# A transfer on SyncE that waits for the last weights is taken out; early stores and dense weights queue behind the values of step 1 instead

## Chip, cores, metric

One Trainium2 chip (trn2), one core. The metric is device time in microseconds (us), the median of several executions; lower is better. Span is the length of the profiled execution alone; it is about 2 us shorter than the time of the same run.

## The reference, cut to what matters

Two kinds of layer, each twice: a recurrent attention layer (A) and a dense layer with relu (B), with residuals.

```python
def _A_ref(x, mem0, Wq, Wk, Wv, Wo, seg_len):      # x: 1 x 2048 x 512, 32 heads of 128
    mem = mem0                                     # 8 rows
    for s in range(n_seg):                         # 64 segments of 32 rows
        h = jnp.concatenate([mem, xs], axis=1)     # 40 rows
        q, k, v = h @ Wq, h @ Wk, h @ Wv           # (written as einsums)
        p = _softmax(where(mask, q k^T * scale, -1e9))
        o = (p v) @ Wo
        mem = o[:, :M, :]                          # the next segment needs it
        outs.append(o[:, M:, :])
x = x + _A_ref(_layernorm(x), ...)
x = x + relu(_layernorm(x) @ w1) @ w2
x = x + _A_ref(_layernorm(x), ...)
x = x + relu(_layernorm(x) @ w1) @ w2
```

The memory makes the segments a chain. The kernel does segment k of the first layer A and segment k - 4 of the second in one *step* k; there are 68 steps. The values of a step are put in place by transfers: its "first values" by two (`V<-vg`), its others by four (`V<-vw`). At the end of every step but the last a VectorE copy (`HT<-st`) puts the new memory where the next step's matmuls read it, so the times of these copies measure the steps.

## The kernel before: the parts that the argument touches

The weights (16 MB of Wq, Wk, Wv, Wo in bf16) are loaded once. The program is a list of operations, which a planner written in the kernel puts in order for each engine, using a table of tuned numbers; the order of each engine is then fixed. The framework that compiles the list places all semaphore waits.

```python
def load_weights():
    for c, p0, n in (...):                       # Wv in 3 parts, then Wq, Wk, Wq, Wk, Wo, Wo
        ...                                      # first part of Wv on SyncE, all others on GpSimd
    def hold():                                  # 32 bytes of the last weights, to a scratch place in DRAM
        nc.sync.dma_start(out=held[:], in_=Wo_sb[0:1, H - 1, 0:16])
    plan.op(SP, 0.78, hold, r=[("W", "o", 2), ("issued", "v", 0)], w=["loaded"], lag=0.0)

def queue(early):                                # who issues: ScalarE early, SyncE later and after "loaded"
    return (ACT, nc.scalar, 0.45, []) if early else (SP, nc.sync, 0.78, ["loaded"])

def prepare_group(g, gate=()):                   # a group is 128 rows of x; groups 1 to 5 are early (EARLY = 5)
    eng, q, t, cond = queue(g <= EARLY)
    def load():
        q.dma_start(out=xb[:, :], in_=A_x[0, 128 * g:128 * (g + 1), :])     # xe: a ring of two buffers
    plan.op(eng, t, load, r=[*cond, *gate], w=[xb], lag=...)
    xnT = layernorm(xb, ...)                     # transposes on PE, copied out by ScalarE or VectorE (xg)
    def put():                                   # the normalised group, kept in DRAM for later
        nc.sync.dma_start(out=xh[g][:], in_=xnT[:, :, :])
    plan.op(SP, 0.5, put, r=[*on(xnT), "loaded"], w=[("xh", g)], lag=3.0)
    if g <= EARLY:
        late_values(g, xnT, range(4))            # x Wv for these rows, before they are due: matmuls "fill<-Wv_sb,xg"
...
load_dense()                                     # w1, w2 of layer B, on SyncE, after "loaded"
for k in range(nsteps):
    ...                                          # load_group, prep_x, step_values, queries_keys, scores, attend,
                                                 # project, place_values, finish_pair (layer B)
```

`held` is a barrier on SyncE: a tiny transfer that reads the last weights, so that everything behind it in SyncE's order waits until they have landed. Its purpose is that stores and later loads do not compete with the weights.

Of the kernel before, what the change touches and what calls it, by code (L numbers as in the profile page):

```python
# [29 lines left out]
RULE = (0.0747, 374.3032, 410609.8064, 1181571967619443.75)  # L30
PERIOD = 67.7026
PLACE = {
    ("attend.mmu0.0", 0): 532.15, ("attend.mmu0.0", 1): -8.807, ("attend.mmu1.0", 0): 515.265,
    ("attend.mmu1.0", 1): 519.958, ("attend.mmu2.0", 0): -268.171, ("attend.mmu2.0", 1): -133.306,
    ("attend.mmu3.0", 0): 161.173, ("attend.mmu3.0", 1): -96.674, ("attend.mmu4.0", 0): -137.041,
    ("attend.mmu4.0", 1): 517.755, ("dense_layer.mm.0", 1): 921.103, ("dense_layer.mm.1", 1): -138.913,
    ("dense_layer.mm.2", 1): -30.48, ("dense_layer.mm.3", 1): 458.108, ("dense_layer.mm.4", 1): -61.608,
    ("dense_layer.mm.5", 1): 915.299, ("finish_pair.turn.0", 1): -801.919, ("g0", 0): -11.927, ("g1", 0): -283.649,
    ("g2", 0): 639.371, ("g3", 0): -139.08, ("g4", 0): 661.02, ("g5", 0): -907.409,
    ("layernorm.turn.0", 1): 227.012, ("layernorm.turn.1", 1): 293.927, ("layernorm.turnr.0", 0): -126.847,  # L40
    ("prepare.turns.0", 0): 540.383, ("project.mm.0", 0): 653.938, ("project.mm.0", 1): 333.318,
    ("project.mm.1", 0): 525.334, ("project.mm.1", 1): 334.98, ("project.mm.2", 0): -82.003,
    ("project.mm.2", 1): 518.149, ("project.mm.3", 0): -40.444, ("project.mm.3", 1): 888.541,
    ("project.mm.4", 0): 246.943, ("project.mm.4", 1): -190.689, ("queries_keys.mmu0.0", 0): -893.01,
    ("queries_keys.mmu0.0", 1): -273.831, ("queries_keys.mmu0.1", 0): -842.026,
    ("queries_keys.mmu0.1", 1): -260.974, ("queries_keys.mmu0.2", 0): -138.796, ("queries_keys.mmu0.2", 1): -4.82,
    ("queries_keys.mmu0.3", 0): -63.064, ("queries_keys.mmu0.3", 1): -125.098, ("queries_keys.mmu1.0", 0): -807.001,
    ("queries_keys.mmu1.0", 1): -900.663, ("queries_keys.mmu1.1", 0): -211.227, ("queries_keys.mmu1.1", 1): -802.87,
    ("queries_keys.mmu1.2", 0): -193.148, ("queries_keys.mmu1.2", 1): -101.071, ("queries_keys.mmu1.3", 0): 111.427,
    ("queries_keys.mmu1.3", 1): -112.736, ("queries_keys.mmu2.0", 0): 372.189, ("queries_keys.mmu2.0", 1): 202.79,  # L50
    ("queries_keys.mmu2.1", 0): 269.477, ("queries_keys.mmu2.1", 1): -102.412, ("queries_keys.mmu2.2", 0): 336.89,
    ("queries_keys.mmu2.2", 1): 125.355, ("queries_keys.mmu2.3", 0): 290.402, ("queries_keys.mmu2.3", 1): 338.394,
    ("queries_keys.mmu3.0", 0): 166.135, ("queries_keys.mmu3.0", 1): 341.493, ("queries_keys.mmu3.1", 0): 263.967,
    ("queries_keys.mmu3.1", 1): 482.48, ("queries_keys.mmu4.0", 0): 524.199, ("queries_keys.mmu4.0", 1): 677.388,
    ("queries_keys.mmu4.1", 0): 454.561, ("queries_keys.mmu4.1", 1): 484.463, ("scores.mmu0.0", 0): -71.985,
    ("scores.mmu0.0", 1): -274.011, ("scores.mmu1.0", 0): 409.078, ("scores.mmu1.0", 1): -990.128,
    ("scores.mmu2.0", 0): -27.329, ("scores.mmu2.0", 1): -82.185, ("scores.mmu3.0", 0): 355.769,
    ("scores.mmu3.0", 1): -114.427, ("scores.mmu4.0", 0): -179.163, ("scores.mmu4.0", 1): -202.683,
    ("scores.turnu0.0", 0): -96.292, ("scores.turnu0.0", 1): 407.69, ("scores.turnu1.0", 0): 458.682,
    ("scores.turnu1.0", 1): 265.886, ("scores.turnu2.0", 0): -824.161, ("scores.turnu2.0", 1): -111.663,  # L60
    ("scores.turnu3.0", 0): -254.322, ("scores.turnu3.0", 1): -268.111, ("scores.turnu4.0", 0): -113.328,
    ("scores.turnu4.0", 1): -181.523, ("values.mm.0", 0): 314.251, ("values.mm.0", 1): 239.343,
    ("values.mm.1", 0): 458.697, ("values.mm.1", 1): -169.069, ("values.mm.2", 0): -66.768,
    ("values.mm.2", 1): 323.729, ("values.mm.3", 0): 571.213, ("values.mm.3", 1): 412.559,
    ("values.mmv0.0", 0): 500.356, ("values.mmv1.0", 0): 434.514, ("values.mmv2.0", 0): 343.318,
    ("values.mmv3.0", 0): 452.783, ("values_narrow.mm.0", 0): -130.097, ("values_narrow.mm.0", 1): -716.386,
    ("values_narrow.mm.1", 0): -612.132, ("values_narrow.mm.1", 1): -220.288,
}
AHEAD = {
    "*bulk.land": -8.095, "*late_values.put": 202.39, "*layernorm.aggr": -92.722, "*layernorm.keep": 142.091,  # L70
    "*layernorm.norm": 249.576, "*layernorm.power": 243.925, "*layernorm.stats": -235.438,
    "*prepare_group.load": -371.102, "*prepare_group.put": 305.32, "*values.ev": -86.818, "attend.ev": -102.918,
    "bulk.land": -139.542, "dense_layer.relu": -63.922, "dense_layer.relu_last": 129.251,
    "finish_pair.add": -261.94, "finish_pair.add0": -215.289, "finish_pair.add1": -256.949,
    "finish_pair.store": 282.199, "finish_pair.widen": 16.832, "late_values.put": 32.946,
    "layernorm.aggr": -276.636, "layernorm.keep": 160.217, "layernorm.norm": -103.511, "layernorm.power": 80.297,
    "layernorm.stats": 44.758, "load_dense.dma1": -59.82, "load_dense.dma2": 248.765, "load_group.get": 110.148,
    "load_group.load": -176.804, "load_weights.dma": -143.99, "load_weights.hold": 53.55, "make_ident": 603.953,
    "make_mask": -111.15, "place_values.dma": -102.564, "prep_x.cp": -256.472, "prepare.get_memory": -96.462,
    "prepare.get_x": 1.615, "prepare.keep": 207.944, "prepare.make_half": -302.762, "prepare.place": -8.736,  # L80
    "prepare.zero": 266.216, "prepare.zero_bank": -152.164, "prepare.zero_columns": 393.537,
    "prepare_group.load": 227.12, "prepare_group.put": -4.216, "project.ev": 251.68, "project.first": 329.265,
    "project.rows": 90.099, "queries_keys.ev": 465.016, "scores.block": 171.381, "scores.exp": 45.003,
    "scores.keep": 73.576, "scores.mul": 297.927, "scores.recip": -327.622, "scores.sub": -127.394,
    "scores.top": -18.285, "scores.total": 62.725, "values.ev": 148.812, "values_narrow.ev": -129.376,
# [213 lines left out]
def kernel(  # L299
# [82 lines left out]
    def load_weights():  # L382

        for c, p0, n in (("v", 0, 1), ("v", 1, 1), ("v", 2, 2), *((c, p0, 2) for cc, p0 in (("qk", 0), ("qk", 2), ("o", 0), ("o", 2)) for c in cc)):
            def dma(c=c, p0=p0, n=n):
                q = nc.gpsimd if (c, p0) != ("v", 0) else nc.sync
                if c == "o":
                    hs = slice(8 * p0, 8 * (p0 + n))
                    q.dma_start(out=Wo_sb[:, hs, :], in_=A_Wo.rearrange("h e d -> e h d")[:, hs, :])
                else:  # L390
                    cs = slice(p0 * PW, (p0 + n) * PW)
                    q.dma_start(out=W_s[c][:, :, cs], in_=W_v[c][:, :, cs])

            bulk(POOL if (c, p0) != ("v", 0) else SP, 0.78, dma, (c, p0), n, w=[("W", c, p0 + i) for i in range(n)],
                 rate=LOAD_O if c == "o" else LOAD)

        def hold():
            nc.sync.dma_start(out=held[:], in_=Wo_sb[0:1, H - 1, 0:16])

        plan.op(SP, 0.78, hold, r=[("W", "o", 2), ("issued", "v", 0)], w=["loaded"], lag=0.0)  # L400

# [53 lines left out]
    held = dram.tile([1, 16], BF, name="held")  # L455
# [91 lines left out]
    hold = [None]  # L547
# [117 lines left out]
    def queue(early):  # L665

        return (ACT, nc.scalar, 0.45, []) if early else (SP, nc.sync, 0.78, ["loaded"])

    def prepare_group(g, gate=()):

        eng, q, t, cond = queue(g <= EARLY)
# [3 lines left out]
        else:  # L675
# [5 lines left out]
            plan.op(eng, t, load, r=[*cond, *gate], w=[xb], lag=SLOW if g <= EARLY else 2.45)  # L681
# [3 lines left out]
        else:  # L685
# [3 lines left out]
            plan.op(SP, 0.5, put, r=[*on(xnT), "loaded"], w=[("xh", g)], lag=3.0)  # L689
# [4 lines left out]
    def load_group(g):  # L694
# [9 lines left out]
        plan.op(SP, 0.78, get, r=["loaded", ("xh", g)], w=[xnT], lag=2.45)  # L704
        plan.op(SP, 0.78, load, r=["loaded"], w=[xb], lag=2.45)
# [89 lines left out]
    def late_values(g, xnT, ps, gate=()):  # L795
# [5 lines left out]
        for p0, n in ((0, 4),) if 0 < g <= min(EARLY, 4) else ((0, 2), (2, 2)):  # L801
# [9 lines left out]
            else:  # L811
                plan.op(SP, 0.78, put, r=["loaded", *[("vg", p) for p in range(p0, p0 + n)]], w=[("vh", g, p0)], lag=4.0)
# [44 lines left out]
    def place_values(k, late):  # L857
# [5 lines left out]
        eng, q, t, cond = queue(k == 0)  # L863
# [316 lines left out]
```

## Time and profile before

| | before |
|---|---|
| median time (the profiled execution, 1661.4 us, not counted) | 1660.28 us (1660.22 to 1660.41, 3 runs) |
| span of the profiled execution | 1659.4 us |
| PE busy | 1595.7 us (96%) |
| longest idle of PE | 26.3 us, from 28.2 to 54.55 us |
| first matmul of step 1 | 82.16 us |

The first view gives busy time by windows: start and end of the stretch, its length, busy us and instructions of PE (TensorE's matmuls), PEld (its weight loads), VectorE (DVE), ScalarE (ACT), GpSimd (POOL), then the granted clock of PE, the share of the DMA engines in use and GB/s.

```profile
core 0: us, PE busy (x) PEld busy (x) DVE busy (x) ACT busy (x) POOL busy (x), PEclk, DMA share, GB/s
30.00:50.00 20.00, 0.00 (x0) 0.00 (x0) 0.00 (x0) 0.00 (x0) 0.00 (x0) 0.50 1.02 360
526.00:1026.00 500.00, 497.09 (x12540) 430.26 (x12537) 356.75 (x947) 328.32 (x803) 41.68 (x100) 1.00 0.11 28
```

In the middle of the kernel PE is busy 99.4%. In the start, no engine computes for 20 us while the weights stream at 360 GB/s.

The waits name who released whom: engine, line and what it wrote, its releaser, total us, times, longest. First PE, ScalarE and SyncE in the first 60 us:

```profile
PE fill L827 <- ACT xg L763: 28.6, 2, 26.3
```

```profile
ACT xg L763 <- DMA held<-Wo_sb: 27.6, 1, 27.6
```

```profile
SPq L398 <- DMA Wo_sb<-in_A_Wo_dram: 51.1, 1, 51.1
```

PE waits for a copy on ScalarE, and that copy for the transfer `held`, although the copy reads nothing of it. The timeline of ScalarE shows how (start, duration, engine; ACTq is ScalarE's queue that issues transfers, in order with its compute):

```profile
25.68 0.59 ACT L763 CAST xg<-fill 128x512 bf16<-128x512 f32 x1
53.52 0.34 ACTq L679 DMA_DIRECT2D xe<-in_A_x_dram  x1
53.91 0.59 ACT L763 CAST xg<-fill 128x512 bf16<-128x512 f32 x1 [27.64 <-DMA held<-Wo_sb]
```

Ahead of the copy stands the issue of a load (L679, x of group 5), and this issue is what waited. The chain that ended last says the same (start, duration, what):

```profile
11.04 41.33 DMA Wo_sb<-in_A_Wo_dram
...
52.39 1.06 DMA held<-Wo_sb
...
53.52 0.34 ACTq L679
...
53.91 0.59 ACT xg L763
...
54.55 1.49 PE fill L827 x4
```

Why does a load of x wait for `held`? The compiled order names the semaphores that each instruction waits for. In it the framework gives the transfers that ScalarE and SyncE issue ("hardware DMAs") eight completion semaphores (DMAHW0 to DMAHW7) in rotation, both queues together: the ninth transfer takes the semaphore of the first, and is not issued until the first has landed. In ScalarE's compiled order, and at the front of SyncE's (not a view of the profile; first number: place in the engine's order):

```
ScalarE  29 L679 DMACopy xe_75<-in_A_x_dram 128x512 [waits DMAHW7_49,DVE_49]
SyncE     2 L398 DMACopy held<-Wo_sb 1x16 [waits DMASW7_49]
SyncE     3 L687 DMACopy xh_108<-xg_68 128x512 [waits DMAHW0_49,DVE_49]
```

`held` is the eighth hardware DMA by this rotation, so it has DMAHW7, and the load of x is the sixteenth. (DMASW7 is the last weight load, on GpSimd.)

At 95.4 us all compute engines stop for 2 us with no releaser ("issue"), while the dense weights load at a DMA share of 1.03:

```profile
97.43 0.57 PE L1046 MATMUL st<-OT,Wo_sb 128*128 128x40 bf16 x16 [2.06 <-issue]
```

### The profile page before, as it was taken

The numbers are of one execution on the slowest core, as the hardware profiler recorded it, in microseconds if no ns is written. First come the engines' busy times: TensorE is split into PE (matmuls) and PEld (weight loads), VectorE is DVE, ScalarE is ACT, GpSimd is POOL, SyncE is SP. The second block draws the span as 40 slices with busy tenths as digits, with TensorE's granted clock in tenths as the row PEclk, the third lists the DMA queues.
The fourth block names the chain that finished last, engine by engine and source line by source line (L and its number), as shares of the span: only waits on it lengthen the run. The fifth ranks groups of instructions, "written<-read, shape, count | busy, mean of one in ns | idle before, by whom it ended". The sixth has DMA issues, their size and how long they took to land.

```text
span 1659.4 us, 89728 instructions
## 1 busy us (share of the span) xinstructions
PE 1595.7 (96%) x40624; PEld 1371.5 (83%) x40624; DVE 1122.4 (68%) x3107; ACT 1049.3 (63%) x2633; POOL 146.1 (9%) x352
## 2 busy tenths in 40 slices
PE   3699999999999999999999999999999999999998
PEld 2478888888888888888888888888888888888886
DVE  3256776677677677767776776676677667766765
ACT  2456676666666666666666666676666666666664
POOL 3101010000000010000000000000000000000000
PEclk8799999999999999999999999999999999999999
DMA  9431101010010111001010101011010010000000
GB/s 356 156 105 28 29 25 31 25 34 22 22 35 24 31 32 25 18 27 35 24 31 25 34 21 31 22 29 32 24 41 18 21 28 26 18 18 19 18 6 7
DMA packets 35488, 64.30 MB, mean 39 GB/s; under 512 B 7226, under 2 KB 19234, under 8 KB 35106
## 3 DMA queue, kind: packets, MB, share of 16 engines
q1 hardware_dynamic: 29218, 39.09, 8.8%
q0 software_dynamic: 4704, 18.35, 3.0%
q8 instruction: 318, 5.21, 1.4%
q10 hardware_dynamic: 1184, 1.12, 0.3%
q14 instruction: 64, 0.52, 0.1%
HBM read 33.50 MB, written 11.93 MB: 27 GB/s over the span
## 4 chain that ended last, share of the span: by engine, by line
PE 93%; DMA 3%; DVE 2%; ACT 1%; issue 1%; POOL 0%; ACTq 0%; POOLq 0%; DVEq 0%
PE work L907 37%; PE st L1046 18%; PE fill L827 16%; PE fill L533 11%; PE work L1019 4%; PE work L936 4%; DMA Wo_sb<-in_A_Wo_dram 2%; PE work L533 2%; ACT OT L763 0%; DVE HT L1062 0%; PE fill L642 0%; DMA xe<-in_A_x_dram 0%; PE fill L846 0%; ACT PT L1000 0%; ACT es L958 0%
## 5 line engine op out<-in xcount | busy, mean ns | idle before, releaser
L907 PE MATMUL work<-HT,Wq_sb 128*128 128x80 bf16 (+1 forms) x8704 | 368.3, 200 | 9.9 <-DVE HT L1062 9.1
L907 PE MATMUL work<-HT,Wk_sb 128*128 128x80 bf16 (+1 forms) x8704 | 363.3, 200 | 0.0
L907 PEld LDWEIGHTS <-Wq_sb 128*128 128x128 bf16 x8704 | 327.5, 99 | 36.2 <-DVE HT L1062 18.7
L1046 PE MATMUL st<-OT,Wo_sb 128*128 128x80 bf16 (+1 forms) x8704 | 340.0, 200 | 3.1 <-issue 2.1
L907 PEld LDWEIGHTS <-Wk_sb 128*128 128x128 bf16 x8704 | 324.8, 100 | 16.8 <-issue 14.6
L1046 PEld LDWEIGHTS <-Wo_sb 128*128 128x128 bf16 x8704 | 320.1, 99 | 8.3 <-issue 5.0
L763 ACT CAST qT<-work 128x320 bf16<-128x320 f32 (+1 forms) x508 | 208.8, 411 | 111.4 <-PE work L907 63.7
L827 PE MATMUL fill<-Wv_sb,HT 128*64 128x512 bf16 x2048 | 259.3, 380 | 0.0
L763 ACT CAST kT<-work 128x320 bf16<-128x320 f32 (+1 forms) x510 | 208.9, 410 | 79.1 <-PE work L907 34.5
L1000 ACT ACTIVATE PT<-work,half 128x320 bf16<-128x320 f32 (+2 forms) x433 | 189.7, 465 | 55.0 <-PE work L533 34.4
L947 DVE TENSOR_TENSOR es<-work,maskb 128x320 f32<-128x320 f32 (+2 forms) x340 | 134.5, 404 | 110.9 <-PE work L936 94.7
L763 ACT CAST OT<-work 128x320 bf16<-128x320 f32 (+1 forms) x382 | 152.1, 415 | 62.7 <-PE work L1019 62.2
L763 ACT CAST vw<-fill 128x512 bf16<-128x512 f32 x204 | 119.3, 585 | 90.1 <-PE fill L827 81.9
L958 ACT ACTIVATE es<-es 128x320 f32<-128x320 f32 (+2 forms) x340 | 138.3, 409 | 42.4 <-DVE es L954 42.0
L954 DVE TENSOR_TENSOR es<-es,mx 128x320 f32<-128x320 f32 (+2 forms) x340 | 146.2, 440 | 4.4
L827 PEld LDWEIGHTS <-HT 128*64 128x64 bf16 x2048 | 97.5, 110 | 59.1
L951 DVE TENSOR_REDUCE mx<-es 128x8 f32<-128x320 f32 (+2 forms) x340 | 132.4, 399 | 4.4
L977 DVE TENSOR_TENSOR P<-es,sm 128x320 bf16<-128x320 f32 (+2 forms) x339 | 132.2, 406 | 3.4
L961 DVE TENSOR_REDUCE sm<-es 128x8 f32<-128x320 f32 (+2 forms) x340 | 131.4, 395 | 2.0 <-ACT es L958 1.9
L1002 DVE TENSOR_SCALAR PT<-work,half 128x320 bf16<-128x320 f32 (+2 forms) x247 | 108.7, 448 | 23.2 <-PE work L533 22.5
L936 PEld LDWEIGHTS <-qT 128*40 128x40 bf16 x4096 | 86.2, 98 | 45.5 <-ACT qT L763 2.4
L1062 DVE CAST HT<-st 128x64 bf16<-128x64 f32 (+1 forms) x67 | 14.8, 221 | 159.5 <-PE st L1046 159.5
(91 smaller groups left out, 1816.6 us busy)
## 6 DMA issues: line engine op xcount, KB each, us to landing
V<-vw SPq DMA_DIRECT2D x252, 48.0 KB
V<-vh SPq DMA_DIRECT2D x120, 64.0 KB
vh<-vg SPq DMA_DIRECT2D x20, 256.0 KB
Wq_sb<-in_A_Wq_dram POOLq DMA_DIRECT2D x2, 2048.0 KB, 22.3
Wk_sb<-in_A_Wk_dram POOLq DMA_DIRECT2D x2, 2048.0 KB, 27.9
Wo_sb<-in_A_Wo_dram POOLq DMA_DIRECT2D x2, 2048.0 KB, 39.2
Wv_sb<-in_A_Wv_dram POOLq DMA_DIRECT2D x1, 2048.0 KB, 11.2
vh<-w_sb POOLq DMA_DIRECT2D x4, 512.0 KB, 4.0
```

Of the source, the lines that this page charges most:

```text
L533: nc.tensor.matmul(out_[u:v, :], lhsT=lhsT[:, u:v], rhs=rhs, start=start, stop=stop, tile_position=(0, u))
L763: nc.scalar.copy(out=out_, in_=in_)
L827: nc.tensor.matmul(vp[64 * b:64 * b + 64, :], lhsT=cols(c4), rhs=Wv_sb[:, c4, n * 512:(n + 1) * 512], start=(c4 == 0), stop=(c4 == NC4 - 1 ...
L907: nc.tensor.matmul(qp[:, hi * 2 * L:hi * 2 * L + n], lhsT=W_sb[:, c4, h * Dh:(h + 1) * Dh], rhs=HT[:, c4, c0:c1], start=(c4 == 0), stop=(c ...
L936: nc.tensor.matmul(v[64 * g2:64 * g2 + L, a, i, b, :], lhsT=qT[:, hi, a * L:(a + 1) * L], rhs=kT[:, hi, a * L:(a + 1) * L], start=True, st ...
L947: nc.vector.tensor_tensor(out=flat(es[:, A]), in0=flat(sp[:, A]), op=ALU.add, in1=maskb[:, a_lo:a_hi, :].unsqueeze(2).to_broadcast([128, n ...
L951: nc.vector.tensor_reduce(out=mx[:, As], in_=es3(), axis=AX.X, op=ALU.max)
L954: nc.vector.tensor_tensor(out=es3(), in0=es3(), op=ALU.subtract, in1=mx[:, As].unsqueeze(2).to_broadcast([128, ns * na, L]))
L958: nc.scalar.activation(out=es[:, A], in_=es[:, A], func=ACTF.Exp, scale=SCALE)
L977: (nc.gpsimd if eng == POOL else nc.vector).tensor_tensor(out=o, in0=flat(es[:, A]), op=ALU.mult, in1=sm[:, As].rearrange("p (a s) -> p a ...
L1000: nc.scalar.activation(out=o, in_=i, func=ACTF.Copy, scale=half[:, b:b + 1])
L1046: nc.tensor.matmul(wo[:, 2 * W * c4 + c0:2 * W * c4 + c1], lhsT=Wo_sb[:, h, c4 * 128:(c4 + 1) * 128], rhs=OT[:, h, c0:c1], start=(h == 0 a ...
```

## The change

Its intent: SyncE is no longer held. `held` goes; "loaded" is now only an order in the plan, written by the last values placed for step 1, and the early stores of xh and the dense weights queue behind these on SyncE. All tuned numbers are new. Core of the diff:

```diff
-RULE = (0.0747, 374.3032, 410609.8064, 1181571967619443.75)
-PERIOD = 67.7026
+RULE = (0.0723, 386.0467, 78079.6446, 1062346643473199.25)
+PERIOD = 75.0294
 ... (some 170 tuned numbers of PLACE and AHEAD, all changed)
-        def hold():
-            nc.sync.dma_start(out=held[:], in_=Wo_sb[0:1, H - 1, 0:16])
-
-        plan.op(SP, 0.78, hold, r=[("W", "o", 2), ("issued", "v", 0)], w=["loaded"], lag=0.0)
-
-        return (ACT, nc.scalar, 0.45, []) if early else (SP, nc.sync, 0.78, ["loaded"])
+        return (ACT, nc.scalar, 0.45) if early else (SP, nc.sync, 0.78)
 ... ("loaded" and cond dropped from the reads of load, get, put and place_values)
-            plan.op(SP, 0.5, put, r=[*on(xnT), "loaded"], w=[("xh", g)], lag=3.0)
+            def put_op(*cond):
+                plan.op(SP, 0.5, put, r=[*on(xnT), *cond], w=[("xh", g)], lag=3.0)
+
+            if g <= EARLY:
+                later.append(put_op)
+            else:
+                put_op()
 ... (place_values: the last transfer of step 1 writes "loaded")
-    plan.mark(2, "s")
-    load_dense()
 ...
-        if 0 in seg and seg[0] % GS == 0 and seg[0] // GS + 1 < NG:
-            load_group(seg[0] // GS + 1)
         step_values(k)
+        if k == 1:
+            for put in later:
+                put("loaded")
+            load_dense()
+        if 0 in seg and seg[0] % GS == 1 and seg[0] // GS + 1 < NG:
+            load_group(seg[0] // GS + 1)
```

## The prediction

> **What bounds the kernel now.** The page shows PE busy 1595.7 of 1659.4 us. From 140 to 1600 us PE is busy over 99%: the steady state is PE-bound, and the change touches no operand there. The start is the exception. By windows PE has no matmul between 30 and 50 us. The waits give one idle of 26.3 us before a values matmul (L827), released by the ScalarE copy `xg`, which waited 27.6 us for "DMA held<-Wo_sb". The chain of waits agrees: last Wo weights to 52.4, `held` to 53.5, a DMA issue on ScalarE's queue (L679, x of group 5) at 53.52, the copy, PE at 54.55.
>
> I read it so: the tiny `held` transfer waits on SyncE for the last weight load. Completion semaphores of hardware DMAs are reused in rotation over eight; in the instruction order ScalarE's third x load waits for the semaphore that `held` took. So ScalarE, and PE behind it, stand still, not only SyncE, though Wk (first half about 28.5 us), Wq (35.4), Wk (40.5) and Wo (46.5; 52.4) land one by one (issue plus time to landing).
>
> **What the change does.** It removes `held`; the same x load then waits for an earlier x load, long done. PE's order at the start is nearly unchanged: the same 192 fills, then Wq, Wk, Wq, Wk, Wo, Wo of 64 matmuls each. Matmuls and row-size changes are equal in number (40,624/887, after 40,615/888). SyncE issues V of step 1 first, then stores of xh and dense weights. The placing numbers are retuned, which reshuffles the steady state; I expect a few us either way.
>
> **Cost.** From 54.55 to 82.16 (first matmul of step 1) PE needed 27.6 us, some 2 us of it from half clock (0.50 until 60 us; the Wk block took 2.31 us, later 1.77) and waits. Against arrivals: Wk from 28.5, fills (0.108 us each), Wq from 35.4, 48 fills to 42.5, Wk to 44.5, 32 fills to 49, Wo to 51, the last Wo block gated by its landing near 52.5 to 53. Step 1 then starts at 55 to 57 us instead of 82.2: 25 to 27 us gained, all on the critical path. Wo's landing becomes the bound, so about 28 is the most.
>
> Losses: PE now runs step 0 under saturated DMA (share 1.02). At 95.4 us before, all compute engines stood still 2 us with no releaser, while the dense weights loaded (DMA 1.03). The Trainium skill, "Runtime: NRT & Kernel Launch", Instruction fetch mechanics, says instruction buffers are refilled in 16 KiB blocks by DMA; this trace agrees: 318 packets, 5.21 MB, 16.4 KB each. I estimate 0 to 3 us more of such stalls, in step 0, or in step 1, where late value stores (2.5 MB) and 2.7 MB of dense weights now meet.
>
> **Prediction.** 1660.3 - 26.5 + 1 = about 1634.5 us, range 1629 to 1641. Faster by over 2%: 0.08; within: 0.91; slower: 0.01.
>
> **What would show it.** No 26 us idle of PE; ScalarE's x load issued near 25 us; PE at work through 30 to 50 us, idle only for landings; chain of waits through Wo landing near 52 to 53; step 1 from 55 to 57; clock 1.00 by then. Dense weights issued near 62, landed by 72. Steady windows at the same 99.4% busy. The last 60 us unchanged, with its 3.3 us wait for a normalised tile.
>
> **What would make it wrong.** Another reused semaphore stalling ScalarE or GpSimd; several instruction-fetch stalls of 2 us under the weight stream; late V of step 1 because stores crowd the engines; a retuned steady state off by over 5 us (0.3% of 1500).

## The result

| | before | after |
|---|---|---|
| median time | 1660.35 us (1660.22 to 1661.48, 4 runs) | 1634.82 us (1634.22 to 1638.11, 4 runs) |
| ratio after/before | | 0.9849, 95% interval 0.9832 to 0.9866 |
| span of the profiled execution | 1659.4 us | 1632.9 us |
| first matmul of step 1 | 82.16 us | 55.33 us |

A ratio is the mean time of one kernel's fast runs over that of the other's of the same rounds, so not quite the ratio of the medians. 1.5% is within the 2% called the same.

The profile after, view by view. Windows: the 20 us without work are now full, and the middle of the kernel is as it was (before 497.09 of 500 us; a few matmul records are missing from the trace after, 40,555 of 40,615, so the busy sum reads a little low).

```profile
30.00:50.00 20.00, 19.82 (x368) 13.80 (x370) 9.20 (x36) 13.07 (x32) 2.25 (x5) 0.91 1.03 375
500.00:1000.00 500.00, 496.13 (x12517) 430.54 (x12534) 357.02 (x948) 327.52 (x801) 41.67 (x100) 1.00 0.10 28
```

PE's longest waits in the first 60 us (the first is the start of the program, where PE has nothing yet; it was 7.1 us before):

```profile
PE fill L488 <- DMA ob<-in_A_mem_dram: 5.9, 1, 5.9
PE work L907 <- DMA Wk_sb<-in_A_Wk_dram: 2.5, 1, 2.5
```

ScalarE issues the load of x for group 5 at 23.67 us instead of 53.52:

```profile
23.67 0.48 ACTq L673 DMA_DIRECT2D xe<-in_A_x_dram  x1
24.03 1.06 ACT L763 CAST qT<-work 128x160 bf16<-128x160 f32 x3
```

The chain that ended last now runs, at the start, through the first half of Wk and then through PE's own work to step 1:

```profile
5.41 24.73 DMA Wk_sb<-in_A_Wk_dram
30.18 2.25 PE work L907 x64
...
52.87 0.29 ACT PT L1000
53.20 0.23 PE work L1019 x2
53.44 1.62 PE st L1046 x64
55.08 0.20 DVE HT L1062
55.33 0.57 PE work L907 x16
...
68.90 2.16 issue
```

Where did the time go? The table gives the time of the memory copy `HT<-st` (start, from the timelines of VectorE) that ends each step. The gain is complete at the end of step 0; 0.76 us of it is given back in steps 1 and 2; from there to the end it moves by less than 0.3 us.

| copy at the end of step | before | after | difference |
|---|---|---|---|
| 0 | 81.91 | 55.08 | -26.83 |
| 1 | 100.39 | 73.92 | -26.47 |
| 2 | 118.90 | 92.83 | -26.07 |
| 3 | 134.76 | 108.70 | -26.06 |
| 16 | 448.04 | 421.94 | -26.10 |
| 48 | 1218.48 | 1192.40 | -26.08 |
| 66 (last) | 1629.56 | 1603.41 | -26.15 |

What remains to be shown is the cause: the reused semaphore (the theory), or SyncE being held as such (rival 1), or the retuned numbers (rival 2).

### The profile page after: what moved, and what is told of

Read it like the earlier page. It is cut to its first block, busy times and chain, and to the rows that moved or that the text cites. A ratio compares the mean times of both kernels' runs of the same rounds, so it can differ in the third digit from the quotient of the medians.

```text
span 1632.9 us, 89617 instructions
## 1 busy us (share of the span) xinstructions
PE 1592.1 (97%) x40555; PEld 1372.8 (84%) x40615; DVE 1124.5 (69%) x3113; ACT 1047.2 (64%) x2625; POOL 147.0 (9%) x354
## 4 chain that ended last, share of the span: by engine, by line
PE 94%; DMA 2%; DVE 2%; ACT 1%; issue 1%; POOL 0%; POOLq 0%; DVEq 0%; ACTq 0%
PE work L907 37%; PE st L1046 19%; PE fill L827 16%; PE fill L527 10%; PE work L1019 4%; PE work L936 4%; PE work L527 2%; DMA Wk_sb<-in_A_Wk_dram 2%; ACT OT L763 1%; DVE HT L1062 0%; PE fill L636 0%; PE fill L846 0%; ACT PT L1000 0%; ACT es L958 0%; DMA V<-vw 0%
```

## The experiments

Twelve runs. Each is timed against the kernel before in the same rounds.

| run | what | time, us | ratio to before |
|---|---|---|---|
| a_lane | before, two stores exchanged on SyncE | 1636.01 | 0.9849 |
| d_hold_first | after, `held` put back ahead of one load | 1662.26 | 1.0004 |
| e_hold_second | after, `held` put back behind that load | 1635.39 | 0.9843 |
| c_oldnum | program of after, numbers of before | 1635.60 | 0.9846 |
| c2_newnum | program of before, numbers of after | 1661.58 | 1.0011 |
| b_nohold | before without `held` | 1636.98 | 0.9860 |
| after2 | after again | 1636.18 | 0.9853 |
| f_split | after, dense weights in two bursts | 1637.62 | 0.9861 |
| g_late | after, dense weights later | 1636.92 | 0.9857 |
| after3 | after again | 1635.76 | 0.9854 |
| h_chunks | after, dense weights in 38 pieces | 1641.63 | 0.9891 |
| i_pieces | after, in 27 pieces, stores first | 1638.46 | 0.9862 |

The intervals are about 0.0015 to each side (2.5 us); c2_newnum has two runs only, and 0.0020. Differences of 1 to 2 us are therefore read from the traces and not from the times.

### a_lane: SyncE still held, but another semaphore

In short:

```diff
+        one, two = [the store of xh of group 1, the store of xh of group 2]
+        # group 1's store goes behind group 2's in SyncE's order
```

> The kernel before with one thing moved: the first two stores of xh on SyncE change places (group 2 ahead of group 1). The held transfer stays, and SyncE still waits for the last Wo weights. By the listing ScalarE's x load of group 5 then reuses the semaphore of an earlier x load and no longer that of held. Theory (a reused completion semaphore stops ScalarE): the idle of 26.3 us on PE is gone, x load issued near 25 us, time 1633 to 1638 although SyncE is still held to about 53 us. Rival 1 (SyncE being held is itself the cost): 1658 to 1662. Rival 2 (the gain is the retuned order): 1658 to 1662.

`held` waits exactly as before, and ScalarE's load no longer does. SyncE's timeline to 56 us, then the load on ScalarE's:

```profile
0.80 0.47 SPq L392 DMA_DIRECT2D Wv_sb<-in_A_Wv_dram  x1
52.28 0.30 SPq L398 DMA_DIRECT2D held<-Wo_sb  x1
```

```profile
25.18 0.49 ACTq L679 DMA_DIRECT2D xe<-in_A_x_dram  x1
```

The longest wait of PE from 20 to 60 us, 26.3 us before, is now

```profile
PE fill L827 <- ACT xg L763: 1.6, 1, 1.6
```

Step 0 ends at 54.13 us, and the time is 1636.01 us, as after. Rival 1 falls: SyncE stands still for 51 us here and it costs nothing that is seen. Rival 2 falls too: every number is the old one. What was exchanged has nothing to do with the load but its place in the rotation: the store of group 2 cannot go before the ScalarE copy that stands just ahead of the load, so with it in front both stores come later in the rotation, behind the load; the load is then one place nearer to `held`, and it reuses the semaphore of an earlier x load (in the compiled order it now waits for DMAHW6).

### d_hold_first and e_hold_second: `held` back in the kernel after, in two places

```diff
 d_hold_first, SyncE's order:  Wv, +held, x of group 1, V of step 1, ...
 e_hold_second, SyncE's order: Wv, x of group 1, +held, V of step 1, ...
```

> The kernel after with the held transfer put back on SyncE, ahead of the x load of group 1 there. By the listing ScalarE's x load of group 5 waits for its semaphore. Theory: the stall of 26 us is back, 1657 to 1664. Rival 2 (the retuned order brought the gain): 1633 to 1637.

> The same transfer put back into the kernel after, one place later on SyncE, behind the x load of group 1. SyncE waits for the Wo weights just as long, but by the listing no ScalarE transfer shares its semaphore. Theory: no stall, 1633.5 to 1637. Rival 1 (SyncE being held is the cost): 1657 to 1664, like d_hold_first.

ScalarE's timeline in d_hold_first, then in e_hold_second, with the same transfer held on SyncE until 52.3 and 52.4 us:

```profile
53.40 0.34 ACTq L674 DMA_DIRECT2D xe<-in_A_x_dram  x1
53.78 0.49 ACT L764 CAST qT<-work 128x160 bf16<-128x160 f32 x2 [29.58 <-DMA held<-Wo_sb]
```

```profile
24.57 0.49 ACTq L674 DMA_DIRECT2D xe<-in_A_x_dram  x1
```

In d_hold_first PE waits behind ScalarE as it did before:

```profile
PE fill L828 <- ACT xg L764: 28.9, 1, 28.9
```

One place in SyncE's order makes 27 us: 1662.26 against 1635.39. The exchange also delays the load of x of group 1, from 1.32 to 52.63 us, but that is not the cause: in a_lane this load comes later still (67.95 us), and there is no such stall. So the barrier itself costs nothing that can be measured here; sharing its semaphore with a transfer that another engine needs is what costs.

### c_oldnum and c2_newnum: what the retuned numbers do

```diff
 c_oldnum:  after, with RULE, PERIOD, PLACE and AHEAD of before
 c2_newnum: before, with RULE, PERIOD, PLACE and AHEAD of after
```

> The program of the kernel after with the placing numbers of before. If the retuned numbers matter little, 1633 to 1637; if they carry a part of the gain, over 1640.

> The program of the kernel before, held transfer and all, with the placing numbers of after. By the listing a ScalarE transfer (second half of the first values of step 0) now waits for the semaphore of held, near 23 us. Theory: stall of 26 to 30 us, 1658 to 1665. If the numbers alone carried the gain: 1633 to 1640.

The old numbers do as well in the new program (0.9846 against 0.9849, 0.9853 and 0.9854 of after), and the new ones gain nothing in the old program. There the rotation hits another transfer, the second half of the first values of step 0, and ScalarE stands at 23 us:

```profile
ACT w_sb L763 <- DMA held<-Wo_sb: 29.3, 1, 29.3
```

### b_nohold: before without `held` alone

```diff
-        plan.op(SP, 0.78, hold, r=[("W", "o", 2), ("issued", "v", 0)], w=["loaded"], lag=0.0)
 ... (and the definitions of hold and held)
```

> The kernel before without the held transfer and nothing else: old numbers, stores of xh early on SyncE, dense weights where they were. Theory: most of the gain, 1634 to 1639; by the listing ScalarE's x load of group 5 now waits for the reading back of group 1's xh, which may land 2 to 3 us later than the load could start, so up to 3 us slower than after2. If the new place of the stores and dense weights carries the gain: over 1645.

1636.98 us: the removal alone carries the gain. The planner now issues the stores of xh early, and the expected small wait is there: ScalarE's load waits for a reading back of xh that has its semaphore, from 26.3 to 28.0 us.

```profile
27.99 0.34 ACTq L673 DMA_DIRECT2D xe<-in_A_x_dram  x1
28.38 0.59 ACT L757 CAST xg<-fill 128x512 bf16<-128x512 f32 x1 [2.09 <-DMA xnA<-xh]
```

Step 0 ends at 55.85 us, against 54.87 in after2. So queueing the stores behind the values of step 1 is worth about 1 us of the trace at most; in the times of the same rounds (0.9860 against 0.9853) it cannot be told from nothing.

### after2, f_split, g_late: the stall that is left near 69 us

The 2 us in which PE waits for nothing that the profile shows is in the kernel before (95.4 us) and after (68.9 us). Both times the dense weights (2752 KB) load.

```diff
 f_split: SyncE's order  ..., w1, ..., first values of step 2, w2, ...     (after: ..., w2, w1, ...)
 g_late:  SyncE's order  ..., first values of step 2, w1, w2, ...
```

> The kernel after once more, as the yardstick of this chip for the next three: 1633 to 1637, with the stall of about 2.2 us near 69 us.

> The kernel after with the dense weights in two goes: w1 where w2 was, near 63 us, and w2 behind the first values of step 2, near 74 us. If the stall of 2.2 us near 69 us is an instruction fetch that waits behind 8 us of dense-weight packets, two bursts of 4 us leave under 1 us of it: 1 to 2 us faster than after2. If it has another cause (the last store of values, the Wo matmuls), it stays at 2 us and the time too.

> The kernel after with all dense weights behind the first values of step 2, near 74 to 83 us. If the stall follows the dense weights, none near 69 us, and one of about 2 us between 76 and 84 us instead; time within 1.5 us of after2, or later if the first dense layer (84.5 us) has to wait. If it belongs to the place in the program, it stays near 69 us.

PE's waits without a releaser between 50 and 110 us, in after2, f_split and g_late:

```profile
PE st L1046 <- issue: 2.8, 2, 2.4
```

```profile
PE work L936 <- issue: 1.9, 1, 1.9
PE st L1046 <- issue: 1.8, 2, 1.3
```

```profile
PE work L936 <- issue: 4.0, 2, 3.0
```

In f_split the stalls are at 69.1 (1.3 us) and 79.8 us (1.9 us); in g_late at 77.4 (0.9 us) and 81.8 us (3.0 us), with none near 69. So the stall follows the dense weights and does not belong to a place in the program. The expectation of f_split, that two bursts of half the length would leave less than 1 us, is a miss: they left 3.3 us.

The trace also has the packets that fetch instructions, 16,384 bytes each. Starts in us near the stalls:

```
after:   57.82  61.33         68.41  74.00  77.54
g_late:  57.35  61.08  64.42  69.19         76.09         82.26
```

While no dense weights load, a fetch comes 3.3 to 4.8 us after the one before; while they load, 7.1 and 5.6 us in the kernel after, 6.9 and 6.2 us in g_late. In these stalls PE stops between 0.5 us before the late packet starts and 0.3 us after it ends, and goes on 1.3 to 1.6 us after its end. The Trainium skill, "DMA: Bandwidth & Descriptors", section "Queues, rings and completion order", says that each DMA engine goes round the queues that have work for it, a packet at a time; no run here shows how a fetch is queued, only that it comes late while the engines are full (share 1.03 to 1.09).

A count in the kept traces (not a view) shows that PE stops because it has run out of instructions. There are 318 such packets for some 81,400 matmuls and weight loads of PE, so 256 to a packet. The first 200 us of all 14 traces have 27 waits of PE of over 0.25 us without a releaser, the longest 3.04 us. In every one of them, the PE instructions started so far, less 256 for each packet that has landed when PE goes on, come to the same number, 193: PE has always stopped at the border of a packet, and goes on 1.2 to 1.6 us after the next one has landed.

Full engines alone do not make a stall. In c_oldnum the dense weights load at a share of 1.07 from 68 to 72 us, and the fetch at 72.1 us comes 7.0 us after the one before, yet PE has no wait of over 0.25 us without a releaser there: the same count is only 139 when that packet lands. In that run PE's clock was at half from 67.2 to 70.6 us, and PE started 342 instructions between these two fetches, against 429 in after's 7.1 us.

A stall costs more than its length, as the granted clock falls behind it. Windows of after2:

```profile
70.00:72.00 2.00, 0.90 (x35) 0.90 (x35) 0.44 (x2) 0.29 (x1) 0.61 (x1) 1.00 1.03 408
72.00:74.00 2.00, 1.71 (x56) 1.53 (x53) 0.46 (x3) 0.29 (x1) 0.00 (x0) 0.74 1.09 370
74.00:76.00 2.00, 2.00 (x50) 1.78 (x46) 0.79 (x2) 0.52 (x2) 0.00 (x0) 0.50 0.56 139
76.00:78.00 2.00, 1.73 (x25) 0.78 (x25) 0.96 (x3) 0.35 (x2) 0.79 (x2) 0.50 0.22 72
78.00:80.00 2.00, 2.00 (x25) 0.52 (x17) 0.33 (x1) 0.58 (x1) 0.00 (x0) 0.56 0.00 0
```

The clock is at half from 72.9 to 79.8 us, for 6.8 us; in the profiles of after and after3 it was so for 3.4 us. Steps 1 and 2 together took 37.75 us in after, 39.56 in after2 and 37.70 in after3, step 3 took 15.9 us in all three. This goes with a part of the scatter of one and the same kernel: after2's span is 1.5 us longer than after's. The span of after3 is 1.3 us longer for another reason: 1.1 us of it lie behind the last copy of the memory, where its clock was at half from 1624.2 us to the end.

### h_chunks and i_pieces: dense weights in pieces

```diff
 h_chunks: w1 as 16 loads of 86 KB (behind the first store of xh), w2 as 22 loads of up to 64 KB
           (10 behind the first values of step 2, 12 behind its others)
 i_pieces: the stores of xh first; w1 as 16 loads; w2 as 11 loads of up to 128 KB (8 and 3)
```

> The kernel after as the yardstick for h_chunks: 1633 to 1638, with a stall of 2 to 2.5 us near 69 us while the dense weights load.

> The kernel after with the dense weights in 38 pieces of 64 to 88 KB on SyncE (16 of w1 near 63 us, 10 of w2 behind the first values of step 2, 12 behind its others), so that issuing (about 0.45 us a piece) and not the engines sets their rate. If the stall is the backlog of dense-weight packets that an instruction fetch waits behind, no stall over 1 us between 60 and 90 us and 1.5 to 3 us faster than after3. Risk: SyncE is busy issuing when values of step 2 are due (72.8 and 79 us), or the last pieces land after 88 us; then equal or slower.

> h_chunks mended: the stores of xh go out before the pieces of w1 (in h_chunks GpSimd waited for them, and PE 3.3 us behind it), and w2 comes in 11 pieces instead of 22, so that the last land before the first w2 matmul. PE, ScalarE and VectorE run the very lists of after. If the backlog of dense-weight packets causes the stall: step 1 in about 16 us (h_chunks 15.96, after3 18.2), step 2 in 18.6 to 19.5 us, ratio to before 0.9825 to 0.984 against 0.985 of after: 1631 to 1634. If SyncE's late issuing costs step 2 again over 2 us: no faster than after.

In both the stall is gone: no wait of PE without a releaser is over 0.4 us from 52 to 110 us, and the fetches come every 3.4 to 4.5 us until about 74 us. Step 1 takes 15.96 and 16.29 us, against 18.23 in after3. This supports the backlog of dense-weight packets as the cause of the late fetches; in what order the DMA engines served them is not shown. But neither is faster, because SyncE pays: issuing takes 0.48 us a piece (median), and what stands behind the pieces is late. In h_chunks GpSimd waits for the stores of xh, and PE behind it; step 2 takes 27.36 us, against 19.47 in after3 (waits of GpSimd, then of PE):

```profile
POOL xg L718 <- DMA xh<-xg: 10.2, 1, 10.2
```

```profile
PE fill L846 <- DVE xg L729: 3.3, 1, 3.3
PE fill L636 <- DMA w_sb<-in_B_w_dram: 2.2, 1, 2.2
```

The second line is PE waiting for the last pieces of w2, until 93.6 us.

In i_pieces that is mended, and the second values of step 2 are issued from 83.7 us on instead of from 79.1; PE waits for them:

```profile
PE work L1019 <- DMA V<-vw: 4.8, 1, 4.8
```

Both expectations of a gain are misses; the risks named in them came true. No version that clearly beats after was found. Issuing the pieces from another engine than SyncE was not tried.

## Why the prediction was right

The time (1634.82 against 1634.5 predicted, range 1629 to 1641) and the mechanism both held.

- **ScalarE's load waits for the semaphore of `held`.** Read from the compiled order, and shown by a_lane, d_hold_first and e_hold_second: with the same barrier on SyncE, 1636.01 and 1635.39 us without the shared semaphore, 1660.62 and 1662.26 with it.
- **25 to 27 us gained, step 1 from 55 to 57 us.** Measured 26.83 us at the end of step 0, and 55.33 us.
- **The last Wo block gated by its landing near 52.5 to 53.** Only nearly. In the profiled run the chain went through the first half of Wk, which landed 24.7 us after its issue, near 30.1 us and not 28.5 (the forecast took the landing of before, where less else was loaded early), and then PE was busy to 52.4 us. In after2 and e_hold_second the Wo block did wait for its weights, 0.4 and 1.0 us. So weights and PE's work end together here, and the two errors of 1.6 us and less did not show in the sum.
- **0 to 3 us more of instruction-fetch stalls.** Booked as 1 us. The stall itself hardly grew (2.06 to 2.16 us); in step 0, under the full weight stream, no matmul waited without a releaser between 24 and 56 us in the profile of after; 0.76 us was given back in steps 1 and 2. The time forecast for the dense weights was a little short: they were issued from 63.4 to 65.1 us (forecast 62), and the engines stayed full until 74 us, not 72.
- **Steady state unchanged within a few us.** It moved by less than 0.3 us from step 3 to step 66, and c_oldnum shows that the new numbers are worth nothing measurable.
- **The last 60 us unchanged.** The 3.3 us wait for a normalised tile is there again.

The sum 26.5 - 1 = 25.5 is what the medians show, 25.5; that it is this close is luck, as the same kernel gave 1634.22 to 1638.11 us. Two slips in the prediction's text change nothing: 1660.3 - 26.5 + 1 is 1634.8 and not 1634.5, and the load of x for group 5 is not ScalarE's third load of x (the trace has the loads of groups 0 to 4 before it) but the third that has to wait for a buffer.

## What to carry to other kernels

When an engine waits for a transfer whose data it does not use, look at the completion semaphores in the compiled order: where a few of them go in rotation over several queues, as here, one long-waiting transfer stops the transfer that comes a full round later, on another queue too, and every instruction behind that. Before removing such a barrier, or after adding one, count the places to the next transfer with its semaphore; exchanging two stores was worth as much here as removing the barrier. And a burst of loads that fills the DMA engines can delay instruction fetches until PE runs out; here, cutting the burst into pieces moved the cost to the queue that had to issue them.

## What the Trainium skill lacked or had wrong

- "DMA: Bandwidth & Descriptors" explains what a completion semaphore counts, but not (nor does any page read for this) that in a compiled program transfers of different queues can share few of them in rotation and so wait for each other: 26 to 30 us of ScalarE and PE here, gone when the place in the rotation moves by one (1662.26 against 1635.39 us).
- "Runtime: NRT & Kernel Launch", section "Instruction fetch mechanics", calls the cost of crossing a 16 KiB boundary mostly hidden. The block size agrees (packets of 16,384 bytes). With the DMA engines full it was not hidden: stalls of 0.9 to 3.0 us in after, f_split and g_late, none over 0.4 us when the same bytes came in pieces (nor in c_oldnum, where PE's clock was low).
- "TensorE: Matmul & The Clock Gate", Part 1, gives an idle window of about 3.4 us for the fall to half clock. The length of the window fits (after these stalls the clock stayed at half for 3.41 or 6.83 us), but the window need not be idle: PE was busy 54% of the 3.41 us before the fall at 72.94 us in after2, 1.8 us after work had resumed, and 37% of those before the fall at 71.36 us in after.
